# Two attention steps interleaved with projections, and a tail whose weight-gradient sums are turned by DMA

## The chip, the cores and the metric

The kernel runs on one core of one Trainium2 chip, in a single launch. The metric is device time in microseconds: the whole execution, a little longer than the span from the first to the last instruction that the profile draws. Lower is better. Numerals such as L157 are lines of the kernel that was profiled, the one from before the change. Engine names follow the profile: PE is the matrix engine, PEld its weight loads, DVE the vector engine, ACT the scalar engine, POOL and SP the two that issue most of the transfers.

## The reference

Forward and backward pass of window attention over a 256 x 256 image of 384 channels in bfloat16, with windows of 8 x 8 tokens:

```python
qkv = xw @ wqkv                                   # xw: windows of 64 tokens, C = 384
q, k, v = qkv[..., :C], qkv[..., C:2*C], qkv[..., 2*C:]
p = softmax(einsum('bqc,bkc->bqk', q, k) * C ** -0.5, axis=-1)
o = einsum('bqk,bkc->bqc', p, v) @ wo
_, vjp = jax.vjp(forward, x, wqkv, wo)
return out, *vjp(grad_out)                        # out, dx, dwqkv, dwo
```

There are 1024 windows. The outputs are the forward result (out_0), the gradient of x (out_1) and the gradients of the two weight matrices (out_2 and out_3).

## The kernel before, in words

The work is cut into 128 quads. A quad is eight windows in a column, held as four tiles of 128 tokens (two windows each). The weights are first multiplied with each other (A = Wq Wk^T times the scale, B = Wv Wo, and their transposes), so that each token needs four products with 384 x 384 matrices: z from the incoming gradient and BT, y from x and A, u from x and B, v from x and AT.

The main loop runs i from 0 to 128, and each pass is a software pipeline over three quads. In pass i, `step(c, b, a, ahead)` handles c = quad i-1 (its attention), b = quad i (its scores, softmax, u and v) and a = quad i+1 (its z and y). All five engines run in the order in which the program lists their instructions, so the text order of `step` is the order on each engine. It is:

1. `scores(b)`, with the softmax pieces `soft(b, 0..4)` on DVE and ACT between eight `uv` products; ACT copies each u and v out of PSUM (L241).
2. Three z products (`project(a, 0, mo)`, three matmuls of 512 columns each, L157), each copied by ACT into the buffer `yz` (L171); then `soft(b, 5)`.
3. `load(ahead)`: the transfers that fetch a later quad (gradients on POOL's queue, x on SP's).
4. `gather(a, 0)`, a DVE copy of z into `zy` (L179), and three y products, copied by ACT (L173).
5. Up to one row of the weight-gradient sums (`gf_rows`), if a group of three finished quads is waiting in the list `fill`. The list is first filled at the end of pass i = 3.
6. For quads 0 to 3 and the last one, `turn(b)` transposes the probabilities on PE and ACT copies them (L252); for the others DVE does it earlier.
7. `attention(c)`: four tiles (`attend`), one per turn of the generator. A tile is twelve half-size matmuls (L283) into banks called pw, pu, po and pd. One pd product reads `tok`, the z and y of quad c turned to token-major form by a DMA transpose on SP's queue (L183), issued by `to_tokens(sts[i])` at the start of pass i, thus one pass before it is used. Copies out of PSUM: W by DVE on even and ACT on odd tiles in the first passes, U by DVE (L297), o by ACT, d by both (L287); POOL then issues the stores. Once `fill` is in use, sixteen half-size matmuls of weight-gradient sums (`gf_halves`, L338) follow each tile. `gather(a, 1)` comes after the second tile.

PSUM has eight banks, one ring. The next pass's `scores` reads all of `yz`, so PE needs the last y copy of ACT before it can finish the scores.

At SP, every pass issues the DMA transposes dT and xT of quad i+2 (L146), then tok of quad i, then the loads of x.

After the loop, `gf_final` adds the last two quads into the sums `GF_acc` (DVE, L320) and casts them to bfloat16 (`final[0]`, `final[1]`; L349), one row of 128 at a time, a generator that `weight_gradients` draws from. `weight_gradients` then forms the four blocks of the weight gradients from them. Two of the blocks need the sums transposed (`GFT`), which `turn_blocks` does: nine PE transposes (L99) and three copies from PSUM (L91, L93) for each of the two. `product_row` makes one row of a block by three matmuls (L418) and one copy.

Of the kernel before, what the change touches and what calls it, by code (L numbers as in the profile page):

```python
# [11 lines left out]
BF16 = mybir.dt.bfloat16  # L12
F32 = mybir.dt.float32

P = 128
# [8 lines left out]
def kernel(  # L24
# [21 lines left out]
    nc = tc.nc  # L46
    _, H, W, C = x.shape
    CK = C // P
# [5 lines left out]
    grp = ctx.enter_context(tc.tile_pool(name="grp", bufs=2 * GQ + 1))  # L54
# [3 lines left out]
    ring = ctx.enter_context(tc.tile_pool(name="ring", bufs=8, space=bass.MemoryType.PSUM))  # L58
# [13 lines left out]
    def columns(k):  # L72
        return slice(k * C, (k + 1) * C)
# [21 lines left out]
    def turn_blocks(dst, src, first=0, act=True):  # L95
        for k in range(CK):
            pt = ring.tile([P, C], BF16, tag="r", name="pt")
            for m in range(CK):
                nc.tensor.transpose(pt[:, m * P:(m + 1) * P], src[:, m, (first + k) * P:(first + k + 1) * P], ident[:])  # L99
            copy_out(k if act else 0, dst[:, k, :], pt[:])  # L100
# [32 lines left out]
    def load(st):  # L133
        st["xq"] = xq = grp.tile([P, QUAD, C], BF16, tag="xq", name="xq", bufs=2 * GQ + 5)
        st["dq"] = dq = qp.tile([P, QUAD, C], BF16, tag="dq", name="dq", bufs=6)
        for t in range(QUAD):
            nc.gpsimd.dma_start(out=dq[:, t, :], in_=windows(grad_out, st, 2 * t))  # L137
        for t in range(QUAD):
            (nc.gpsimd if st["i"] == AHEAD + 1 else nc.sync).dma_start(out=xq[:, t, :], in_=windows(x, st, 2 * t))
# [21 lines left out]
    def project(st, kind, mo):  # L161
        if kind == 0 and mo == 0:
            st["yz"] = qp.tile([P, CK, QUAD, 4, WT], BF16, tag="yz", name="yz", bufs=1)
        yz = st["yz"]
        wgt, src = ((BT_sb, st["dT"]), (A_sb, st["xT"]))[kind]
        pj = ring.tile([P, QUAD, 2, WT], F32, tag="r")
        for m in range(CK):
            product(pj[:].rearrange("p t w k -> p (t w k)"), wgt[:, m, mo * P:(mo + 1) * P], src[:, :, m, :],
                    m == 0, m == CK - 1)
        if kind == 0:  # L170
            ENG[EV["z"][mo]](out=yz[:, mo, :, 0:4:3, :], in_=pj[:])  # L171
        else:
            ENG[EV["y"][mo]](out=yz[:, mo, :, 1:3, :], in_=pj[:])  # L173
# [24 lines left out]
    def soft(st, step):  # L198
        sd = st["sd"]
        if step == 0:  # L200
            st["mx"] = mx = sm.tile([P, QUAD], F32, tag="mx", name="mx")
            for w, h in ((0, HI), (1, LO)):
                nc.vector.tensor_reduce(out=mx[h, :], in_=sd[h, :, w, :], axis=AX.X, op=ALU.max)
        elif step == 1:
            mx = st["mx"]
            st["sh"] = sh = sm.tile([P, QUAD, WT], F32, tag="sh", name="sh")
            for w, h, o in ((0, HI, LO), (1, LO, HI)):
                nc.vector.tensor_tensor(out=sh[o, :, :], in0=sd[h, :, w, :], in1=over_k(mx[h, :], WT),
                                        op=ALU.subtract)
        elif step == 2:  # L210
            st["ex"] = ex = sm.tile([P, QUAD, WT], F32, tag="ex", name="ex")
            nc.scalar.activation(out=ex[:], in_=st["sh"][:], func=ACT.Exp)
        elif step == 3:
            ex = st["ex"]
            rs = sm.tile([P, QUAD], F32, tag="rs")
            nc.vector.tensor_reduce(out=rs[:], in_=ex[:], axis=AX.X, op=ALU.add)
            ri = sm.tile([P, QUAD], F32, tag="ri")
            nc.vector.reciprocal(out=ri[:], in_=rs[:])
            st["ps"] = ps = qp.tile([P, 2, QUAD, WT], BF16, tag="ps", name="ps")
            st["Pb"], st["dS"] = ps[:, 0, :, :], ps[:, 1, :, :]  # L220
            nc.vector.tensor_tensor(out=st["Pb"], in0=ex[:], in1=over_k(ri[:]), op=ALU.mult)
        elif step == 4:
            st["pr"] = pr = sm.tile([P, QUAD, WT], F32, tag="pr", name="pr")
            for w, h in ((0, LO), (1, HI)):
                nc.vector.tensor_tensor(out=pr[h, :, :], in0=sd[h, :, w, :], in1=st["Pb"][h, :, :], op=ALU.mult)
            st["D"] = D = sm.tile([P, QUAD], F32, tag="D", name="D")
            nc.vector.tensor_reduce(out=D[:], in_=pr[:], axis=AX.X, op=ALU.add)
        else:
            pd = sm.tile([P, QUAD, WT], F32, tag="pd")
            nc.vector.tensor_tensor(out=pd[:], in0=st["Pb"], in1=over_k(st["D"][:]), op=ALU.mult)  # L230
            nc.vector.tensor_tensor(out=st["dS"], in0=st["pr"][:], in1=pd[:], op=ALU.subtract)
# [120 lines left out]
    def attention(st):  # L352
        halves = gf_halves(*fill.pop(0)) if fill else iter(())
        for t in range(QUAD):
            attend(st, t)
            yield
            for k in range(QUAD):
                next(halves, None)

    def step(c, b, a, ahead):  # L360


        def on(st):
            return (lambda f, *r: f(st, *r)) if st is not None else (lambda f, *r: None)
        C_, B, A = on(c), on(b), on(a)
        B(scores)
        B(soft, 0)
        B(uv, 0, 0)
        B(uv, 0, 1)
        B(soft, 1)  # L370
        B(uv, 1, 0)
        B(uv, 1, 1)
        B(soft, 2)
        B(soft, 3)
        B(uv, 2, 0)
        B(uv, 2, 1)
        B(uv, 3, 0)
        B(uv, 3, 1)
        B(soft, 4)
        for mo in range(CK):  # L380
            A(project, 0, mo)
        B(soft, 5)
        if b is not None and not b["on_pe"]:
            turn(b)
        if b is not None and b["i"] == 1:
            turn_blocks(woT_sb, wo_sb, act=False)
        if ahead is not None:
            load(ahead)
        A(gather, 0)
        for mo in range(CK):  # L390
            A(project, 1, mo)
        for rows in range(1 if a is not None else 2):
            if fill:
                gf_rows(*fill.pop(0))
        if b is not None and b["on_pe"]:
            turn(b)
        slots = attention(c) if c is not None else iter(())
        for t in range(QUAD):
            if t == 2:
                A(gather, 1)  # L400
            next(slots, None)
        for rest in slots:
            pass
# [8 lines left out]
    dwo_out = out_3.rearrange("(m p) n -> p m n", p=P)  # L412

    def weight_gradients(group):
        def product_row(k, out, left, right, sc):
            pe = ring.tile([P, C], F32, tag="r", name="pe")
            for m in range(CK):
                nc.tensor.matmul(pe[:], lhsT=left[:, m, k * P:(k + 1) * P], rhs=right[:, m, :],  # L418
                                 start=(m == 0), stop=(m == CK - 1))
            if sc is not None and k % 2:  # L420
                nc.scalar.activation(out=out, in_=pe[:], func=ACT.Copy, scale=sc)
            elif sc is not None:
                nc.vector.tensor_scalar(out=out, in0=pe[:], scalar1=sc, scalar2=None, op0=ALU.mult)
            else:
                copy_out(k, out, pe[:])

        def rows(name):
            return grp.tile([P, CK, C], BF16, tag="xq", name=name, bufs=2 * GQ + 5)

        GFT = [grp.tile([P, CK, C], BF16, tag="Wq", name="GFT") for f in range(2)]  # L430
        for i in range(CK + 1):
            next(group)
        turn_blocks(GFT[0], final[0])
        for i in range(CK - 1):
            next(group)
        for part, left, right in ((0, GFT[0], w_sb[:, :, columns(1)]), (1, final[0], w_sb[:, :, columns(0)])):
            dw = rows("dw")
            for k in range(CK):
                product_row(k, dw[:, k, :], left, right, scale)
            nc.sync.dma_start(out=dw_out[:, :, columns(part)], in_=dw[:])  # L440
        turn_blocks(GFT[1], final[1])
        dwo = rows("dwo")
        for k in range(CK):
            product_row(k, dwo[:, k, :], w_sb[:, :, columns(2)], final[1], None)
        nc.sync.dma_start(out=dwo_out, in_=dwo[:])
        dw = rows("dw")
        for k in range(CK):
            product_row(k, dw[:, k, :], GFT[1], woT_sb, None)
            (nc.sync, nc.scalar)[k % 2].dma_start(out=dw_out[:, k, columns(2)], in_=dw[:, k, :])

    with tc.manual_schedule(engines=MANUAL):
        spare = sm.tile([P, 1], BF16, name="spare", bufs=1)
# [77 lines left out]
```

## Time and profile before

| what | value |
|---|---|
| three timed runs | 1898.62, 1900.75, 1900.82 us (median 1900.75) |
| the profiled execution, its own time | 1902.77 us |
| its span in the profile | 1901.0 us |
| granted PE clock, mean | 0.999 |
| pass i = 2, scores to scores: length, PE busy, ACT busy, DVE busy | 12.73, 11.95, 11.56, 9.85 us |
| pass i = 3: the same | 12.74, 11.95, 11.56, 9.86 us |
| pass i = 4 (the sums now run too): the same | 14.56, 14.56, 11.66, 12.67 us |
| 1887.60 to 1897.30, the products of the tail: length, PE busy, DMA share | 9.70, 9.64 us, 0.19 |

The length of a pass is read in the timeline from the first scores matmul of one pass to the first of the next; the busy times are those of the same stretch. A PE that is busy over a whole stretch leaves no time to be gained from other engines there; where it is less, something makes it wait. The DMA share is the mean busy share of the sixteen transfer engines, with overlapping packets counted twice, so it can pass 1.

### The profile page before, as it was taken

To read this page: it belongs to the slowest core of one execution; us is meant where nothing else is said; L and a number is where in the kernel's file an instruction comes from. 1 tells how busy PE (TensorE), PEld (TensorE's weight loads), DVE (VectorE), ACT (ScalarE), POOL (GpSimd) and SP (SyncE) were. 2 spreads that over 40 slices of the span, in tenths; PEclk is the share of its full clock that TensorE was granted. 3 is DMA by queue.
4 is the path that set the end of the run, shared out by engine and by line. 5 is a ranking of instruction groups with operands and counts; after the bars stand their busy time and mean duration, and the time that the engine had idled before them with its cause. 6 is when DMAs were issued, how large, how long until landed. Compare 5 with 4: busy or idle time off the path is not lost.

```text
span 1901.0 us, 57224 instructions
## 1 busy us (share of the span) xinstructions
PE 1890.5 (99%) x22413; PEld 1128.2 (59%) x22413; DVE 1664.8 (88%) x3606; ACT 1524.7 (80%) x3347; POOL 863.1 (45%) x1576
## 2 busy tenths in 40 slices
PE   9999999999999999999999999999999999999999
PEld 5555565566556655665556655655565566556655
DVE  6888888888888888888888888888888888888887
ACT  7888788878888887888778887888788878888884
POOL 4544454445444444454444444444444445444532
PEclk9999999999999999999999999999999999999999
DMA  9999999999999999999999999999999999999994
GB/s 223 239 219 225 219 217 216 212 224 217 216 221 201 234 216 216 226 216 218 182 231 217 220 220 208 228 209 224 214 216 223 218 207 233 203 230 220 217 185 96
DMA packets 946543, 407.69 MB, mean 214 GB/s; under 512 B 828512, under 2 KB 921696, under 8 KB 946272
## 3 DMA queue, kind: packets, MB, share of 16 engines
q1 hardware_dynamic: 869760, 252.04, 78.4%
q0 software_dynamic: 75264, 151.11, 31.3%
q8 instruction: 175, 2.87, 0.6%
q10 hardware_dynamic: 1248, 0.89, 0.2%
q14 instruction: 96, 0.79, 0.1%
HBM read 101.84 MB, written 101.84 MB: 107 GB/s over the span
## 4 chain that ended last, share of the span: by engine, by line
PE 98%; DMA 1%; DVE 1%; ACT 0%; issue 0%; ACTq 0%; DVEq 0%
PE pj L157 52%; PE pg L157 13%; PE ph L338 13%; PE sd L157 5%; PE pw L283 5%; PE po L283 4%; PE pu L283 4%; DMA tok<-zy 1%; PE pd L283 1%; PE pe L418 0%; DVE Uq L297 0%; PE pc L106 0%; DMA w_sb<-in_wqkv_dram 0%; DVE Wq L294 0%; DVE zy L179 0%; PE pt L99 0%
## 5 line engine op out<-in xcount | busy, mean ns | idle before, releaser
L303 POOL DMA_DIRECT2D out_dram<-o x512 | 273.6, 534 | 918.2 <-ACT o L287 901.9
L294 ACT CAST Wq<-pw 128x384 bf16<-128x384 f32 x506 | 243.4, 481 | 279.5 <-PE pw L283 279.2
L157 PEld LDWEIGHTS <-xT 128*128 128x128 bf16 x3072 | 291.8, 98 | 182.2
L157 PE MATMUL pj<-B_sb,xT 128*128 128x384 bf16 x1536 | 333.4, 326 | 0.0
L157 PE MATMUL pj<-AT_sb,xT 128*128 128x384 bf16 x1536 | 333.3, 326 | 0.0
L137 POOL DMA_DIRECT2D dq<-in_grad_out_dram x508 | 269.1, 542 | 77.7 <-PE pj L157 30.3
L297 DVE CAST Uq<-pu 128x384 bf16<-128x384 f32 x512 | 283.0, 553 | 14.8 <-PE pu L283 2.6
L305 POOL DMA_DIRECT2D out_dram<-d x480 | 278.8, 581 | 15.2 <-ACT uq L241 5.1
L157 PE MATMUL pj<-dT,BT_sb 128*128 128x512 bf16 x1152 | 269.5, 379 | 0.1
L157 PE MATMUL pj<-xT,A_sb 128*128 128x512 bf16 x1152 | 269.5, 379 | 0.0
L283 PE MATMUL pd<-tok,ps 64*64 64x384 bf16 x2048 | 255.1, 327 | 2.3 <-DMA tok<-zy 2.3
L171 ACT CAST yz<-pj 128x512 bf16<-128x512 f32 x384 | 224.3, 585 | 38.4 <-PE pj L157 29.6
L287 ACT CAST o<-po 128x384 bf16<-128x384 f32 x512 | 249.9, 488 | 2.2 <-PE po L283 2.1
L241 ACT CAST vq<-pj 128x384 bf16<-128x384 f32 x512 | 246.6, 482 | 3.6
L241 ACT CAST uq<-pj 128x384 bf16<-128x384 f32 x512 | 243.7, 476 | 3.8 <-PE pj L157 1.9
L173 ACT CAST yz<-pj 128x512 bf16<-128x512 f32 x384 | 224.7, 585 | 24.5 <-PE pj L157 0.6
L258 DVE STREAM_TRANSPOSE PS<-ps 32x256 bf16<-32x256 bf16 x492 | 214.4, 436 | 9.4
L157 PEld LDWEIGHTS <-xq 128*128 128x128 bf16 x1572 | 153.6, 98 | 115.3 <-issue 0.9
L338 PEld LDWEIGHTS <-xq 64*64 64x64 bf16 x6000 | 176.7, 107 | 68.1
L338 PE MATMUL ph<-Wq,xq 64*64 64x384 bf16 x3984 | 204.2, 322 | 0.0
L157 PEld LDWEIGHTS <-A_sb 128*128 128x128 bf16 x1152 | 112.6, 98 | 135.5
L157 PEld LDWEIGHTS <-BT_sb 128*128 128x128 bf16 x1152 | 112.7, 98 | 122.3
(95 smaller groups left out, 3058.2 us busy)
## 6 DMA issues: line engine op xcount, KB each, us to landing
out_dram<-o POOLq DMA_DIRECT2D x512, 96.0 KB, 3.9
xq<-in_x_dram SPq DMA_DIRECT2D x508, 96.0 KB, 4.1
dq<-in_grad_out_dram POOLq DMA_DIRECT2D x508, 96.0 KB, 5.9
out_dram<-d POOLq DMA_DIRECT2D x480, 96.0 KB, 4.3
out_dram<-d POOLq DMA_DIRECT2D x64, 48.0 KB, 4.8
tok<-zy SPq DMA_TRANSPOSE x128, 7.7
xT<-xq SPq DMA_TRANSPOSE x127, 7.5
dT<-dq SPq DMA_TRANSPOSE x126, 7.6
```

What stands on the lines that cost most here:

```text
L137: nc.gpsimd.dma_start(out=dq[:, t, :], in_=windows(grad_out, st, 2 * t))
L157: nc.tensor.matmul(out, lhsT=lhsT, rhs=rhs, start=start, stop=stop)
L171: ENG[EV["z"][mo]](out=yz[:, mo, :, 0:4:3, :], in_=pj[:])
L173: ENG[EV["y"][mo]](out=yz[:, mo, :, 1:3, :], in_=pj[:])
L241: cp(out=dst[:, t, :], in_=pj[:])
L283: nc.tensor.matmul(dst[o, :], lhsT=operand(st, lhs, t, h), rhs=operand(st, rhs, t, h), **flags)
L287: copies[EV[name][i]](out=sb[rows, :], in_=src[rows, :])
L294: copies[EV["W"][t] if st["i"] >= GQ else "DA"[t % 2]](out=st["Wq"][:, t, :], in_=pw[:])
L297: copies[EV["U"][t]](out=st["Uq"][:, t, :], in_=pu[:])
L303: nc.gpsimd.dma_start(out=windows(out_0, st, 2 * t), in_=o)
L305: nc.gpsimd.dma_start(out=windows(out_1, st, 2 * t - 1), in_=d if t else above[:])
L338: nc.tensor.matmul(dst[o, :], lhsT=st["xq"][h, t, ma * P + o.start:ma * P + o.stop], rhs=st["UW"[f] + "q"][h, t, :], start=(i == 0), stop= ...
```

## The change

In passes i = 2 and i = 3 (c is quad 1 or 2) `step` takes a path of its own after `soft(b, 4)`: `load(ahead)` first, then one attention tile of c after each of the three z products and after the first y product; `soft(b, 5)` behind the second z product's tile; `gather(a, 0)` behind the third tile; the other two y products, `turn(b)` and `gather(a, 1)` at the end. Each of the operations that the two passes had is still there, once.

In the tail, each of the two transposed sums is made by one DMA transpose on SP's queue instead of `turn_blocks`. The block that needs no transposed sum is formed first. The last of the twelve rows is formed in two halves of 192 columns, one copied by ACT and the other by DVE, and stored by SP.

```diff
@@ step, after B(soft, 4)
+        if c is not None and c["i"] in (1, 2):
+            load(ahead)
+            slots = attention(c)
+            for mo in range(CK):
+                project(a, 0, mo)
+                next(slots)
+                if mo == 1:
+                    soft(b, 5)
+            gather(a, 0)
+            project(a, 1, 0)
+            next(slots)
+            project(a, 1, 1)
+            project(a, 1, 2)
+            for rest in slots:
+                pass
+            turn(b)
+            gather(a, 1)
+            return
         for mo in range(CK):
             A(project, 0, mo)
@@ weight_gradients
+        def turned(src):
+            dst = grp.tile([P, CK, C], BF16, tag="Wq", name="GFT")
+            nc.sync.dma_start_transpose(out=dst[:].rearrange("p m (k q) -> p (m k) q", q=P),
+                                        in_=src[:].rearrange("p m c -> p (m c)"))
+            return lambda m, k: dst[:, k, m * P:(m + 1) * P]
+
+        def plain(src):
+            return lambda m, k: src[:, m, k * P:(k + 1) * P]
...
-        GFT = [grp.tile([P, CK, C], BF16, tag="Wq", name="GFT") for f in range(2)]
-        for i in range(CK + 1):
+        for i in range(CK):
             next(group)
-        turn_blocks(GFT[0], final[0])
-        for i in range(CK - 1):
+        GFT = [turned(final[0])]
+        for i in range(CK):
             next(group)
-        for part, left, right in ((0, GFT[0], w_sb[:, :, columns(1)]), (1, final[0], w_sb[:, :, columns(0)])):
+        GFT.append(turned(final[1]))
+        for part, left, right in ((1, plain(final[0]), w_sb[:, :, columns(0)]), (0, GFT[0], w_sb[:, :, columns(1)])):
...
-        turn_blocks(GFT[1], final[1])
...
-        for k in range(CK):
+        for k in range(CK - 1):
             product_row(k, dw[:, k, :], GFT[1], woT_sb, None)
             (nc.sync, nc.scalar)[k % 2].dma_start(out=dw_out[:, k, columns(2)], in_=dw[:, k, :])
+        for part, put in ((0, nc.scalar.copy), (1, nc.vector.tensor_copy)):
+            half = slice(part * C // 2, (part + 1) * C // 2)
+            pe = ring.tile([P, C // 2], F32, tag="r", name="pe")
+            for m in range(CK):
+                nc.tensor.matmul(pe[:], lhsT=GFT[1](m, CK - 1), rhs=woT_sb[:, m, half],
+                                 start=(m == 0), stop=(m == CK - 1))
+            put(out=dw[:, CK - 1, half], in_=pe[:])
+        nc.sync.dma_start(out=dw_out[:, CK - 1, columns(2)], in_=dw[:, CK - 1, :])
```

More of the change, by code (lines that the diff above doesn't have):

```diff
@@ L417, in product_row @@
             for m in range(CK):
-                nc.tensor.matmul(pe[:], lhsT=left[:, m, k * P:(k + 1) * P], rhs=right[:, m, :],
+                nc.tensor.matmul(pe[:], lhsT=left(m, k), rhs=right[:, m, :],
                                  start=(m == 0), stop=(m == CK - 1))
@@ L440, in weight_gradients @@
             nc.sync.dma_start(out=dw_out[:, :, columns(part)], in_=dw[:])
-        turn_blocks(GFT[1], final[1])
         dwo = rows("dwo")
         for k in range(CK):
-            product_row(k, dwo[:, k, :], w_sb[:, :, columns(2)], final[1], None)
+            product_row(k, dwo[:, k, :], plain(w_sb[:, :, columns(2)]), final[1], None)
         nc.sync.dma_start(out=dwo_out, in_=dwo[:])
         dw = rows("dw")
-        for k in range(CK):
+        for k in range(CK - 1):
             product_row(k, dw[:, k, :], GFT[1], woT_sb, None)
             (nc.sync, nc.scalar)[k % 2].dma_start(out=dw_out[:, k, columns(2)], in_=dw[:, k, :])
+        for part, put in ((0, nc.scalar.copy), (1, nc.vector.tensor_copy)):
[6 more added lines that the diff above has]
+        nc.sync.dma_start(out=dw_out[:, CK - 1, columns(2)], in_=dw[:, CK - 1, :])
     with tc.manual_schedule(engines=MANUAL):
```

## The prediction, made before the changed kernel ran

> **What bounds the kernel.** I read the chain of waits first: it runs on PE.
>
> ```profile
> PE 98%; DMA 1%; DVE 1%; ACT 0%; issue 0%; ACTq 0%; DVEq 0%
> ```
>
> Then I looked for PE's waits, in the list of PE's waits and the timeline. From pass i = 4 on there is one alone, at 949.8 us, so only passes 1 to 3 and the tail can give anything. Pass i = 2, from scores to scores, reads:
>
> ```profile
> 39.50 0.87 PE L157 MATMUL sd<-xT,yz 128*128 128x64 bf16 x24
> 44.11 2.11 PE L157 MATMUL pj<-dT,BT_sb 128*128 128x512 bf16 x9
> 51.01 0.32 PE L283 MATMUL pw<-dq,ps 64*64 64x384 bf16 x1 [0.23 <-DVE Uq L297]
> 51.95 0.32 PE L283 MATMUL po<-uq,PS 64*64 64x384 bf16 x1 [0.41 <-DVE Wq L294]
> 52.23 0.87 PE L157 MATMUL sd<-xT,yz 128*128 128x64 bf16 x24
> ```
>
> The four tiles run from 48.28 to 52.23, at the speed of the copies; where PE is undisturbed a tile takes 0.49 (pw starts at 76.67, ph behind it at 77.16). Four would take 1.96, so about 2 us are lost here, and as much in pass i = 3. Third, the transfer that feeds those tiles, tok of quad 1, in SP's timeline and in the answer for that transfer (from issue to landing):
>
> ```profile
> 36.75 4.89 SPq L183 DMA_TRANSPOSE tok<-zy  x1
> DMA to landing us min/median/max: 9.7/9.7/9.7
> ```
>
> It lands at 46.45, which is 1.8 before its first use at 48.28. For quad 2 (issued 48.26, 8.8 to landing) it is 57.06 against 61.01. The tail:
>
> ```profile
> 1887.62 0.67 PE L99 MATMUL pt<-ident,GFb 128*128 128x128 bf16 x9
> 1891.52 0.36 DVE L349 CAST GFb<-GF_acc 128x384 bf16<-128x384 f32 x1
> 1893.65 0.67 PE L99 MATMUL pt<-ident,GFb 128*128 128x128 bf16 x9
> 1895.62 1.63 PE L418 MATMUL pe<-woT_sb,GFT 128*128 128x384 bf16 x9
> 1897.28 0.56 DVE L93 CAST dw<-pe 128x384 bf16<-128x384 f32 x1 [0.42 <-PE pe L418]
> ```
>
> PE never stops there: each group of nine transposes costs 0.50 of PE (their start to the next group's).
>
> **Change 1, passes i = 2 and 3.** Nothing is added or removed; PE's sum per pass is scores and u, v 4.61 (39.50 to 44.11), z and y 9 + 9 matmuls at 0.216 = 3.89, the turn 0.31, tiles 1.96: 10.8 against 12.73. At best each pass gains 1.9.
>
> First wait, tok. In pass 2 PE reaches tile 0 after the first z product, 44.11 + 0.65 = 44.76. Everything up to there is as before, on SP too, whose order in these passes isn't changed, so tok lands at 46.45 again: PE waits 1.7 at pd, and behind it stands all of PE, so ACT and DVE run dry as well. In pass 3 tok of quad 2 (57.06) is in time: PE needs it 5.3 after that pass's start, about 58.5.
>
> Second wait, the end of the pass. Today ACT finishes the last o and d under the next pass's scores, which don't need them; now the last y copies come last, and the scores do need them. ACT's spacing when it has a backlog: 0.37 for a 384-column copy (49.16, 49.53, 49.90), 0.48 for one of 512 (the last y copy at 48.20, PS behind it at 48.68). Pass 2 after the wait: PE has tiles 1.96, five products 3.24, turn 0.31 = 5.5, to 52.0. ACT gets its first o at 46.5 + 0.49 + 0.15 = 47.1, and has 4 o, 2 W and 3 d at 0.37 = 3.3 and five z and y at 0.48 = 2.4; with 0.1 for the end of the last and 0.3 to 0.6 where it waits for PE, 53.2 to 53.5. The scores begin in earnest 1.0 to 1.3 later than 52.23; I take 1.2.
>
> That PE stops there is seen at the start of passes 0 and 1, where z and y also come straight before the scores, in the chain:
>
> ```profile
> 25.54 0.59 ACT yz L173
> 26.14 0.05 issue
> 26.18 0.82 PE sd L157 x22
> ```
>
> Pass 3 has no tok wait, but the same end. ACT's z0 copy comes 5.5 after the scores (52.23 to 57.75 today), behind it 6 at 0.48 and 9 at 0.37 = 6.2: 11.8 if it never runs dry, today 12.74. But it does: the second z product ends 0.49 + 0.65 after the first, DVE (four U, two W, two d, `soft(b, 5)`, two gathers: ten at 0.47 and 0.9 = 5.6) holds banks, and each tile's po waits for u's copy. I put 0.5 to 1.3 for it, so -0.4 to +0.4, and take +0.2. What hides today's copies, the next scores and u, v, is gone for y2; DVE's `gather(a, 1)` now follows y2 and holds back the next maximum by 0.5, which PE doesn't wait for (u and v run meanwhile).
>
> POOL issues `dq` before the stores as before; the stores come 2 to 3 earlier, and o has eight buffers. Cost nothing; were a store late by a pass, ACT would wait for it. Passes 4 onward are PE's own, so a shift of the front stays to the end: **+1.4**, between -3.8 (1.9 twice: nothing waits) and +2.5 (all of tok's 1.7 lost, and 0.4 in each pass).
>
> **Change 2, the tail.** Out go 18 PE transposes (2 x 0.50 = -1.0) and six copies, which lay beside PE. In come two DMA transposes of 9 blocks. Nearest row, 12 blocks on a less loaded queue:
>
> ```profile
> 33.35 1.44 SPq L146 DMA_TRANSPOSE dT<-dq  x1
> DMA to landing us min/median/max: 3.8/3.8/3.8
> ```
>
> Bounds: 2.3 (a plain store of the same 288 KB) and 7.6 (the median dT, under load). The tail's DMA share is 0.19, so I go by 3.8 less three blocks; tok's 24 blocks against dT's 12 at their median give only 0.1 for 12, which makes no useful slope, so I take 3.3 to 3.8, 3.5. First transpose: `final[0]` ready 1887.48, lands 1891.0. PE: two sum rows to 1890.39, the plain block 1.46 to 1891.85; hidden, with 0.8 to spare. Second: cast ends 1891.88 - 0.5 = 1891.38, lands 1894.9; PE has block 0 and dwo, 2.92, to 1894.77. Wait 0.1. The last block starts at 1894.9 instead of 1895.62.
>
> The halves: in row 1 ACT copies (0.48), issues a store (0.37 at 1897.30) and only then copies the half row. From the last block's start: row 1 done 0.97 + 0.18, copy 0.49, store issue 0.4, half copy 0.32 (0.48 less 192 columns at 0.84 ns, from 384 and 512 columns' 0.478 and 0.585): 2.4 until SP issues, against 2.25 today. +0.15. Tail: -0.72 + 0.15, **-0.6**, between -0.8 and the third case below.
>
> Sum: +1.4 - 0.6 = **+0.8** on the span of 1901.0, so 1901.8, and 1903.6 for that execution's own 1902.77. Its median companion is 1900.75, 2.0 lower, and the lowest run 1898.62. The reason is in the trace: tok at 936.78 landed 15.27 later, PE stood 2.30, and then a window ran at half clock.
>
> ```profile
> 950.02:953.43 3.41, 1.34 (x31) 0.82 (x32) 1.26 (x3) 0.86 (x2) 0.00 (x0) 1.00 1.06 205
> 953.43:956.85 3.42, 3.42 (x44) 2.24 (x47) 2.13 (x5) 1.82 (x4) 2.48 (x4) 0.50 1.18 260
> ```
>
> (Columns: length, busy of PE, PEld, DVE, ACT, POOL, granted clock, DMA share, GB/s.) 2.3 + 1.7 = 4.0, about 1902.77 - 1898.62: a late transfer that not every run has. The forecast is the median plus 0.8: **1901.5**.
>
> **Rivals.**
> A. *The copies do hide* (faster). Both passes reach PE's sum: -3.8, tail -0.6: 1896.4. For it: with a backlog ACT needs 17 copies at 0.37, 7 at 0.48 and 0.3 for the exponential, 10.0, and DVE is busy 9.85; both are under 10.8. Against: tok's landing, and y2 last.
> B. *Half of that*: pass 2 loses its 1.2, pass 3 gains 1.9: -1.3, 1899.4. For it: in pass 3 only the order of the copies stands in the way.
> C. *The turned sums are late* (slower). One mechanism: the transposes take the loaded 7.6. The first lands 1895.1, PE waits 3.2 and ends dwo at 1898.0; the second lands 1899.0, the last block starts 3.4 later than today; tail +3.5, total 1905.7. It decides from about 4.0 for the second transpose, where the tail stops gaining. Against: the idle queue. The Trainium skill (VectorE: DVE Perf Modes, The three transpose paths) prefers TensorE where PSUM will do, 390 ns a block, and puts the DMA path at 1309 ns; nine in a row would be an estimate of 11.8, both behind each other on one queue, the last block 15.5 late, 1918. The row of 12 blocks in 3.8 speaks against blocks in a row.
> D. *The new wait halves the clock*. 1.7 of standing in pass 2 is followed by a 3.4 window at 0.50, as above: +1.7, 1903.2. Against: the window before that one had PE busy 1.34 of 3.41; 1.7 of waiting leaves half or more. The Trainium skill (TensorE: Matmul & The Clock Gate, Part 1: The HAM clock gate) asks for an idle window of about 3.4 us, free-running; by that no gate closes here, though at 949.8 a 2.3 wait was enough.
>
> **How the numbers follow.** Forecast 0.58, A 0.10, B 0.12, C 0.10, D 0.10. The forecast's own range is 1900.5 to 1902.2 (pass 2 +1.0 to +1.3, pass 3 -0.4 to +0.4, tail -0.8 to -0.3); runs with and without the late transfer differ by 2.2, so 1898.3 to 1904.4 holds it with B and D, and leaves out A and C. What a measurement can tell from no change is about 0.2%, 3.8 us: beyond it lie on the fast side A (0.10), on the slow side C and D with a late transfer on top (0.13); the rest, 0.77, is no change.
>
> **What would show it.** Right: a PE wait at pd for tok of 1.5 to 1.9 near 44.8 to 46.5; scores of pass 4 starting 1.0 to 2.0 later than 64.97, waiting for ACT yz; passes after that at 14.57; the transposes of GFb landing in 3 to 4; the last block's first matmul 5.4 to 5.7 before the end (today 5.4). Wrong: no wait for tok, passes under 12, or a wait over 1 at GFT.

## The result, and the profile after

The changed kernel's median is 1901.49 us (22 runs, 1899.08 to 1905.87). The kernel before, run beside it on the same chip, has 1898.68 (22 runs, 1898.11 to 1901.54). The ratio is 1.0016, with a 95% interval of 1.0009 to 1.0022: some 3.0 us slower (1.7 to 4.2), which is within what was called no change, but on its slow side and clear of zero. The forecast of 1901.5 agrees with the time only because two errors cancel. It stood on a median of three runs, 1900.75, two of which were untypical (18 of the 22 runs of the kernel before lie between 1898.1 and 1899.3), and it added 0.8 where 2.8 was right. That the two errors met is luck.

The profiled execution has a span of 1901.0 us, just as the one before. But that of before had lost time to a late transfer at 949.8. The pass that holds it goes from one of these scores to the other:

```profile
938.90 0.87 PE L157 MATMUL sd<-xT,yz 128*128 128x64 bf16 x24
958.00 0.87 PE L157 MATMUL sd<-xT,yz 128*128 128x64 bf16 x24
```

It takes 19.10, where the passes around it take 14.57, thus 4.5 more (the prediction had reckoned 4.0). Without it, 1896.5 is what the new span should be held against. The chain of waits gives the same picture as before:

```profile
PE 98%; DMA 1%; DVE 0%; ACT 0%; issue 0%; ACTq 0%
```

So PE's waits are next. These are two lines of the list of what PE waited for: total us, times, longest.

```profile
PE pd L283 <- DMA tok<-zy: 3.2, 1, 3.2
PE sd L157 <- ACT yz L173: 0.6, 2, 0.3
```

The first is a transfer, the second the y copy at the end of the two changed passes. The timeline of PE says where they lie (start, duration, what ran; in brackets the idle time before it and its cause):

```profile
40.14 0.87 PE L157 MATMUL sd<-xT,yz 128*128 128x64 bf16 x24
...
45.51 0.35 PE L283 MATMUL pd<-tok,ps 64*64 64x384 bf16 x2
...
52.33 0.38 PE L157 MATMUL sd<-xT,yz 128*128 128x64 bf16 x2
52.99 0.82 PE L157 MATMUL sd<-xT,yz 128*128 128x64 bf16 x22 [0.28 <-ACT yz L173]
...
61.81 0.53 PE L283 MATMUL pd<-tok,ps 64*64 64x384 bf16 x2 [3.18 <-DMA tok<-zy]
...
69.75 0.55 PE L157 MATMUL sd<-xT,yz 128*128 128x64 bf16 x2
70.58 0.81 PE L157 MATMUL sd<-xT,yz 128*128 128x64 bf16 x22 [0.28 <-ACT yz L173]
...
85.08 0.87 PE L157 MATMUL sd<-xT,yz 128*128 128x64 bf16 x24
```

A pass is the distance from one start of the scores (`sd`) to the next. Pass 2 takes 52.33 - 40.14 = 12.19, pass 3 takes 17.42, pass 4 takes 15.33; before, they were 12.73, 12.74 and 14.56. Pass 3 holds a wait of 3.18 at pd, and no wait stands in pass 2, where the prediction had put one. (The 0.6 is 0.28 in front of the 22 late scores of pass 3 and 0.28 in front of those of pass 4. What follows the scores, the first u product, starts 0.71 after their start in pass 2, 1.31 in pass 3 and 1.48 in pass 4.) SP's timeline and the answer for the transfer that PE waited for, tok of quad 2:

```profile
36.52 4.20 SPq L183 DMA_TRANSPOSE tok<-zy  x1
47.74 7.01 SPq L183 DMA_TRANSPOSE tok<-zy  x1
```

```profile
DMA to landing us min/median/max: 14.0/14.0/14.0
```

It was issued at 47.74, half a us earlier than before, and took 14.0 where it had taken 8.8. What moved most in its time are the stores. The first of pass 2, in POOL's timeline, starts 6.89 after that pass's first scores (first line); before, it was 10.45 after (second line, from the profile before):

```profile
47.03 0.55 POOL L303 DMA_DIRECT2D out_dram<-o  x1 [0.44 <-ACT o L287]
49.95 0.54 POOL L303 DMA_DIRECT2D out_dram<-o  x1 [2.92 <-ACT o L287]
```

The last part of pass 3 is the clock. These are two windows in a row; the columns are length, busy time of PE, PEld, DVE, ACT and POOL, granted clock, DMA share, GB/s:

```profile
58.19:61.61 3.42, 0.44 (x2) 0.10 (x1) 0.83 (x2) 0.62 (x2) 0.52 (x1) 1.00 1.05 185
61.61:65.02 3.41, 3.21 (x26) 1.02 (x26) 1.58 (x3) 1.09 (x3) 1.08 (x2) 0.50 1.21 248
```

PE was busy for 0.44 of the first, and in the second it got half the clock. Pass 3 is 5.23 longer than pass 2, and the timeline splits this in three. The scores are 0.60 late. From their late end to the first pd it takes 3.51 more (the 3.18 of the list counts only from the end of the product before). From pd to the end of the pass it takes 69.75 - 61.81 = 7.94, where pass 2 takes 52.33 - 45.51 = 6.82; these 1.12 hold the window at half clock, which thus cost less than the 1.7 that half of a whole window would be.

The tail, in the timeline:

```profile
1888.55 5.18 SPq L435 DMA_TRANSPOSE GFT<-GFb  x2
...
1892.70 1.63 PE L445 MATMUL pe<-w_sb,GFT 128*128 128x384 bf16 x9
...
1894.16 1.62 PE L445 MATMUL pe<-GFb,w_sb 128*128 128x384 bf16 x9
...
1895.72 1.15 PE L445 MATMUL pe<-woT_sb,GFT 128*128 128x384 bf16 x6
...
1896.70 0.66 PE L480 MATMUL pe<-woT_sb,GFT 128*128 128x192 bf16 x6
...
1897.41 0.36 ACTq L475 DMA_DIRECT2D out_dram<-dw  x1
...
1897.82 0.32 ACT L482 CAST dw<-pe 128x192 bf16<-128x192 f32 x1 [0.44 <-ACT dw L91]
1898.16 0.34 SPq L483 DMA_DIRECT2D out_dram<-dw  x1
```

The two transposes were issued 3.90 apart and each landed after 3.2, at 1891.8 and 1895.7. PE came to the first sum at 1892.70, after it had landed, and to the second at 1895.72. That is 1.56 after the block before it, where the blocks ahead are 1.46 apart, so PE lost 0.10. From the last pass's scores to the end it is 38.93, against 39.93 before.

The clock column of the single runs says how often the windows at half clock come. One such window in a span of 1900 takes the mean clock to 0.999. Of the 22 runs of the changed kernel 11 have 0.999 or less, with a median of 1902.82; the other 11 have 1.000 and 1901.05, still 2.4 above the kernel before, so the clock is the smaller part of the loss. Of 111 runs of the kernel before, made beside the experiments, 8 have 0.999 or less.

### The profile page after: what moved, and what is told of

It is laid out like the page before. It is cut to its first block, busy times and chain, and to the rows that moved or that the text cites. A ratio compares the mean times of both kernels' runs of the same rounds, so it can differ in the third digit from the quotient of the medians.

```text
span 1901.0 us, 57195 instructions
## 1 busy us (share of the span) xinstructions
PE 1891.0 (99%) x22398; PEld 1125.1 (59%) x22398; DVE 1662.6 (87%) x3602; ACT 1523.0 (80%) x3346; POOL 861.8 (45%) x1576
## 4 chain that ended last, share of the span: by engine, by line
PE 98%; DMA 1%; DVE 0%; ACT 0%; issue 0%; ACTq 0%
PE pj L157 52%; PE pg L157 13%; PE ph L338 13%; PE sd L157 5%; PE pw L283 5%; PE po L283 4%; PE pu L283 4%; DMA tok<-zy 1%; PE pd L283 1%; PE pe L445 0%; PE pc L106 0%; PE warm L87 0%; PE pt L99 0%; ACT yz L173 0%; DVE Uq L297 0%; PE pt L153 0%
```

## The experiments

They run from the two halves of the change to the transfers. The time beside each is the median; "before" is the kernel before on the same chip.

**The tail alone (e1), and the passes alone (e2).** First the new tail without the path in `step`, then that path with the old tail:

```diff
-        if c is not None and c["i"] in (1, 2):
+        if c is not None and c["i"] in ():
```

> The tail of the change alone; passes i = 2 and 3 as before. Late-tok theory (the loss is PE waiting at pd for the transfer tok in passes 2 and 3, and the half clock that can follow): about 0.7 us faster than before, no PE wait at pd in passes 2 and 3, runs as close together as those of before. Rival 'the turned sums are late': slower than before by up to 3 us, PE waiting at a product that reads GFT. Rival 'last y copy': as the first.

> The interleaved passes alone; tail as before. Late-tok theory: 3 to 4 us slower than before in the median, runs spread over some 6 us, and in the profile the time of passes 2 and 3 beyond before's 25.5 equals PE's wait at pd for tok plus about 1.7 for each window at half clock. Rival 'last y copy': slower by a fixed 1 to 2 us, with PE waiting for ACT yz at the two scores, whatever tok does.

The tail alone gives 1897.46 against 1898.75 before, 0.9995 (0.9987 to 1.0004); 10 of 11 runs lie between 1896.9 and 1898.1, and its tail measures 38.94, 1.0 shorter. The interval doesn't show the gain, but the same 38.93 to 38.97 stands in the profile of each of the twelve kernels with the new tail, and 39.93 and 39.94 in the two with the old. The passes alone give 1901.82, 1.0013 (1.0004 to 1.0022): they carry the whole loss. In their profile PE waits 1.78 for tok of quad 2, which took 12.6, and these are the window that holds that wait and the one behind it:

```profile
57.05:60.47 3.42, 1.64 (x16) 0.57 (x15) 1.62 (x4) 1.06 (x3) 0.34 (x1) 1.00 1.37 251
60.47:63.88 3.41, 3.41 (x18) 0.80 (x16) 2.53 (x6) 2.29 (x5) 1.37 (x3) 0.50 0.97 213
```

**tok issued first (e3, e4).** In passes 1 and 2, SP issues tok of quad i, which the next pass reads, ahead of dT and xT of quad i+2; once in the changed kernel, once with the old order of `step` (both with the new tail).

```diff
+            if i in (1, 2):
+                to_tokens(sts[i])
             load_turn(...)
-            if 0 <= i < n:
+            if 0 <= i < n and i not in (1, 2):
                 to_tokens(sts[i])
```

> The changed kernel, with tok issued ahead of the transposes dT and xT in passes 1 and 2, so that it goes out some 3 to 5 us earlier on SP's queue. Late-tok theory: no wait at pd in passes 2 and 3, no half clock, 2.5 to 4 us faster than the changed kernel, 0 to 1 us faster than before; spread of runs as before's. Rival 'last y copy': only the tok part goes, still 1 us or more slower than before. A new wait could come at the z products of passes 2 and 3, which read dT.

> As the run before this one (tok first, new tail), but with passes 2 and 3 in the order of before. Tells what the interleaving is worth when tok is not late. Late-tok theory with the copies as the bound: the same time as with the interleaving within 1 us, about 0.7 us faster than before, passes 2 and 3 at 12.7 each. If interleaving hides the copies: 2 to 4 us slower than the interleaved one.

The changed kernel comes to 1901.66, 1.0016 (1.0007 to 1.0024), the plain one to 1898.96, 1.0000 (0.9991 to 1.0009), 1.5 more than the tail alone. Nothing was won. PE's waits in the changed kernel with tok first:

```profile
PE pd L283 <- DMA tok<-zy: 2.4, 2, 2.2
PE pj L157 <- DMA dT<-dq: 2.4, 2, 2.0
PE pj L157 <- DMA xT<-xq: 0.8, 1, 0.8
```

The longest ones came later in the queue: 2.0 for dT of quad 4, which now stood behind tok of quad 2, and 2.2 for tok of quad 3. (The 0.8 for xT and the other 0.4 for dT lie in passes 0 and 1, ahead of the edit.) In the plain one tok of quad 2 took 13.4, without early stores, while dT and xT moved beside it. This speaks for a shortage in the whole stream of these passes, and not in one place of the queue. The two long waits left the clock alone: the windows around them have PE busy 1.96 and more.

```profile
56.77:60.19 3.42, 1.96 (x13) 0.98 (x10) 2.29 (x6) 2.46 (x7) 2.33 (x5) 1.00 1.28 175
60.19:63.60 3.41, 2.90 (x31) 1.06 (x32) 1.68 (x4) 1.74 (x4) 0.55 (x1) 1.00 1.15 248
77.25:80.66 3.41, 2.34 (x14) 1.13 (x12) 1.04 (x3) 0.68 (x2) 0.00 (x0) 1.00 1.19 124
80.66:84.08 3.42, 2.14 (x47) 1.32 (x51) 2.14 (x4) 1.34 (x3) 0.55 (x1) 1.00 1.22 242
```

**The stores held (e5), and the last tile behind y (e8).** POOL collects the stores of quads 1 and 2 and issues them at the end of the pass's text, behind a small POOL copy that reads the first y copy. The second version also moves the fourth tile behind the last y product, so that the y copies no longer come last.

```diff
+    def store(st, out, in_):
+        if st["i"] in (1, 2):
+            late.append((out, in_))
+        else:
+            nc.gpsimd.dma_start(out=out, in_=in_)
...
-        nc.gpsimd.dma_start(out=windows(out_0, st, 2 * t), in_=o)
+        store(st, windows(out_0, st, 2 * t), o)
...
             project(a, 1, 0)
-            next(slots)                 # second version alone
...
             gather(a, 1)
+            nc.gpsimd.tensor_copy(out=spare[:], in_=a["yz"][:, 0, 0, 1, 0:1])
+            for out, in_ in late:
+                nc.gpsimd.dma_start(out=out, in_=in_)
+            late.clear()
             return
```

> The changed kernel, with POOL's stores of passes 2 and 3 held back until the first y copy of the pass, some 10 us after its scores, where they stood before the change; everything else as changed. 'Early stores' theory (the stores of o and d, now 3 us earlier, share the transfer engines with tok of quad 2 and make it take 13 to 14 us instead of 9): tok of quad 2 takes 8 to 10 again, no or under 1 us of PE wait at pd in pass 3, no half clock, 2.5 to 4 us faster than the changed kernel, 0.5 to 1 faster than before. Rival 'tok is just needed too early': tok of quad 2 still 12 or more, PE waits 1 us or more in pass 3, still 2 us slower than before. In both PE waits some 0.4 for ACT yz at each of the two following scores.

> As the first of these four (stores held), and the fourth tile goes behind the third y product instead of the first, so that ACT copies y2 before that tile's o and d. If the last y copy holds the scores, PE's waits for ACT yz go, passes 2 and 3 take 11.3 to 12.0 each, and the kernel is 2 to 3 us faster than before. If the two passes are bound by their copies alone, 12.2 to 12.7 each and no gain over the first of the four.

With the stores held, tok of quad 2 lands in 6.3 instead of 14.0:

```profile
DMA to landing us min/median/max: 6.3/6.3/6.3
```

This execution flatters it, for in it PE had stood in pass 2 (below), which may have left the transfers more time. The second version had no such wait: there the first store of pass 2 starts 10.63 after the scores, close to the 10.45 of before, and tok of quad 2 takes 8.3, close to the 8.8 of before. So in this order it is the early stores that lengthen it, as far as one execution each can show. The time is still 1901.48, 1.0007 (0.9996 to 1.0018), in two groups: 4 runs at 1898.0 to 1898.8 and 8 at 1901.05 and above. The profile is one of the upper group, and there it is tok of quad 1, which PE meets in pass 2, that comes late; PE's waits and the window:

```profile
PE pd L291 <- DMA tok<-zy: 2.5, 1, 2.5
```

```profile
47.68:51.09 3.41, 1.39 (x18) 0.50 (x19) 0.99 (x2) 0.48 (x1) 1.03 (x2) 1.00 1.18 201
```

That is the wait that the prediction had in pass 2, and the half-clock window of its rival D behind it. It was there in this execution and not in that of the changed kernel, although the program ahead of it is the same: it is a matter of the single run.

The second version has the lowest ratio of the study, 0.9988 (0.9978 to 0.9998). Its median is 1897.9 against 1898.78: 0.9 less, where the tail alone has 1.3 less, so the medians show no gain from the passes. PE in its profile:

```profile
39.67 0.87 PE L157 MATMUL sd<-xT,yz 128*128 128x64 bf16 x24
...
51.48 0.87 PE L157 MATMUL sd<-xT,yz 128*128 128x64 bf16 x24
...
63.28 0.87 PE L157 MATMUL sd<-xT,yz 128*128 128x64 bf16 x24
...
77.84 0.87 PE L157 MATMUL sd<-xT,yz 128*128 128x64 bf16 x24
...
92.41 0.87 PE L157 MATMUL sd<-xT,yz 128*128 128x64 bf16 x24
...
104.75 0.35 PE L291 MATMUL pd<-tok,ps 64*64 64x384 bf16 x2 [1.46 <-DMA tok<-zy]
...
109.23 0.87 PE L157 MATMUL sd<-xT,yz 128*128 128x64 bf16 x24
```

The 24 scores run in one piece, no y copy is waited for, and passes 2 to 4 take 11.81, 11.80 and 14.56, in sum 38.17 where the kernel before has 40.03: 1.9 gained, half of the 3.8 that PE's sum allowed. The last three lines show where it went: in pass 6 PE waits 1.46 for tok of quad 5, which took 13.0, and the pass takes 16.82, 2.3 more than its neighbours. In this execution the front's gain was lost again, and more.

**One pass alone (e6, e7).** The condition becomes `c["i"] == 2` (pass 3 alone) and `c["i"] == 1` (pass 2 alone).

> The changed kernel with pass 2 in the order of before; pass 3 interleaved; new tail. 'Early stores': pass 2's stores are where they were, so tok of quad 2 takes 8 to 10 and PE waits under 0.5 in pass 3; 0.5 to 1 faster than before. 'Needed too early': PE waits 1 us or more at pd in pass 3 and the time is 1 us or more over that of the tail alone.

> The changed kernel with pass 3 in the order of before; pass 2 interleaved; new tail. 'Early stores': tok of quad 2 takes 12 to 14, but is needed 3.4 later, so a wait at pd in pass 3 of 0 to 1; about the time of the tail alone, up to 1 over it. 'Needed too early': no wait at all, tok at 8 to 10.

Medians 1898.38, 0.9994 (0.9984 to 1.0004), and 1899.16, 0.9998 (0.9987 to 1.0008). With the new tail worth -1.0 in both, either pass alone costs nothing to 1.4. It doesn't settle which of the two carries the loss. The profiles do say how the stores bear on tok of quad 2: 14.2 where pass 2 stores early, 11.3 where it stores as before. With pass 3 alone, PE waits 1.9 for it, and the window behind this one has half the clock:

```profile
57.75:61.16 3.41, 1.51 (x16) 0.57 (x15) 1.50 (x4) 0.93 (x3) 1.84 (x4) 1.00 1.16 251
```

**Without reading tok (e9).** In quads 1 and 2 the product that reads `tok` reads the tiles dq and xq instead, which are there long before; that part of out_1 is another value then.

```diff
     def operand(st, n, t, h):
...
+        if n in ("z", "y") and st["i"] in (1, 2):
+            return st[{"z": "dq", "y": "xq"}[n]][h, t, :]
```

> The changed kernel, in which the attention of quads 1 and 2 takes the two tok operands from the tiles of the gradient and of x that the same attention tile reads anyway, so it waits for no turned z and y (those two quads' part of out_1 is not the reference's). Same matmuls, same copies; tok is still moved. Late-tok theory: no wait at pd in passes 2 and 3, passes 12.2, 12.2 and 15.3, no half clock, 3 to 4 us faster than the changed kernel, about 1.3 faster than before, runs as close together as before's. Rival 'the copies and the last y are the loss': still 1 us or more slower than before.

Its profiled execution has no wait for a transfer at all, and a span of 1895.4 (1897.15 in time, the fastest of its runs). Its passes 2 to 4 take 12.19, 12.79 and 15.16, in sum 40.14, as long as before's 40.03: with nothing late, this order of tiles gains nothing, since each pass ends in the wait for y. But the median of the 12 runs is 1900.35, 1.0010 (0.9997 to 1.0022), up to 1912.01. So the theory that the reading of tok in passes 2 and 3 is the whole loss falls. The clock column agrees: the run of 1912.01 has 0.997 and that of 1903.6 has 0.999, so PE stood somewhere in them too.

**Other orders (e10, e11).** One puts all three z products first and a tile behind each y product; the other puts z and the first y product first.

```diff
             for mo in range(CK):
                 project(a, 0, mo)
-                next(slots)
-                if mo == 1:
-                    soft(b, 5)
+            soft(b, 5)
+            next(slots)                 # second version: behind project(a, 1, 0)
             gather(a, 0)
-            project(a, 1, 0)
-            next(slots)
-            project(a, 1, 1)
-            project(a, 1, 2)
+            for mo in range(CK):        # second version: a tile behind the middle one alone
+                project(a, 1, mo)
+                next(slots, None)
```

> Computes all. In passes 2 and 3 the three z products come first, then the tiles, each behind which one y product: tile 0 needs tok 1.3 us later than in the changed kernel, and y2 stands ahead of the fourth tile. Late-tok theory: waits at pd rarer and smaller than in the changed kernel but not gone, passes 11.5 to 12.0 without a wait; median 1 to 2 us faster than before, with some runs 3 slower. If the loss had been in the copies alone: every run 2 faster than before.

> Computes all. As the one above, but a y product more ahead of tile 0, which needs tok 1.9 us later than in the changed kernel and 1.6 earlier than before; stores come 1.6 earlier than before. Late-tok theory: hardly a wait, passes 11.6 to 12.0, 2 to 3 us faster than before in the median and the least spread of all interleaved kernels.

They come to 1899.97, 1.0002 (0.9993 to 1.0010), with waits of 0.4, 1.3 and 0.6 at pd, and 1900.21, 1.0009 (0.9999 to 1.0019), whose profiled execution, at 1896.7 the second fastest, lists no wait of PE for a transfer and has passes 2 to 4 of 38.57 in sum, 1.6 less than e9's, but whose runs go from 1896.23 to 1907.22. In an execution where nothing is late, a tile behind the last y product is thus worth what the wait for y had cost; over all runs the gain is not there.

**Without reading tok, quads 1 to 9 (e12).** The same edit as above, for nine quads.

> As the kernel that read no tok for quads 1 and 2, but for quads 1 to 9 (those quads' part of out_1 is not the reference's). The time of that one stayed spread from 1897 to 1912 although passes 2 and 3 could not wait for tok. 'The wait moves to a later tok' (PE, being earlier, uses up what the transfers had to spare, and stands at tok in passes 4 to 10 instead): now nearly all runs within 1 us of 1897.3, 1.3 to 1.5 faster than before. Rival 'it moves to another transfer' (dT or xT in front of the projections): the runs stay spread over 5 us or more, the median 1 us or more above before, and a slow execution's profile has PE waiting for dT or xT.

The median is 1901.77, 1.0006 (0.9997 to 1.0016). No product of these quads reads tok any more, and still PE stands. DVE's timeline in pass 4, and PE's:

```profile
79.40 0.56 DVE L179 COPY zy<-yz 128x1536 bf16<-128x1536 bf16 x1 [3.38 <-DMA tok<-zy]
80.00 0.56 DVE L322 TENSOR_TENSOR GF_acc<-pg,GF_acc 128x384 f32<-128x384 f32 x1
```

```profile
80.61 0.32 PE L285 MATMUL pw<-dq,ps 64*64 64x384 bf16 x1 [2.31 <-DVE GF_acc L322]
```

The transfer tok of quad 3 was still made, took 13.8, and still read the buffer `zy`. DVE's gather of the next z had to wait 3.38 for that buffer, the sum `GF_acc` stood behind it on DVE and held a bank, and PE waited 2.31 for the bank. PE's list of waits names DVE there, but the cause is the transfer. So neither expectation holds as it was put: the time doesn't fall to 1897.3, and PE waits for neither dT nor xT. The clock followed:

```profile
77.90:81.31 3.41, 0.99 (x24) 0.45 (x20) 1.84 (x4) 0.63 (x2) 0.55 (x1) 1.00 1.19 232
81.31:84.72 3.41, 3.41 (x49) 2.62 (x45) 2.34 (x5) 2.00 (x5) 1.92 (x3) 0.50 1.18 176
```

**What the runs say together.** The stream of transfers in the first passes has little to spare. Before the change, tok of quads 1 to 4 landed 1.8, 4.0, 6.1 and 7.9 before its first use; in the changed kernel's profile it is 0.0, none (3.18 late), 7.2 and 12.0, the last two only because PE had stood. The interleaving takes from this twice: PE needs tok some 3.4 earlier in the pass (8.78 after its start before, 5.37 in pass 2 now), and the stores, which come 3.5 earlier too, lengthen it from about 9 to between 11 and 15. The profiles show executions that lose nothing, a wait, or a wait and a halved window; which of these a given run meets seems to be decided by small differences between runs. The middle twelve of the 22 runs of the changed kernel cover 1.85 us, those of the kernel before 0.65. (The extremes tell less: among the runs of the kernel before that stand beside the experiments, single ones reach 1906.39.)

Left open: only one run of each kernel was profiled, so where the late ones of e9, e10 and e11 stood is not shown. The profiles show where the single executions lost their time; that late transfers make up the whole 3 us of the medians is argued from them. Holding the stores alone left the median at 1901.48, and reading no tok left it at 1900.35 and 1901.77. The one version that brought it back, to 1897.9, holds the stores and moves the fourth tile as well; between it and the held stores alone lies only that tile's place, worth 3.6 in the medians, of which the wait for y explains 2.0 (passes 2 to 4 of 40.14 in e9 against 38.17). Nor was it tried whether lighter traffic in the first passes makes the 1895 to 1896 of the best single runs the rule.

## Why the prediction was right and wrong

**Bound, right for this kernel.** PE sets the time, and in the changed kernel's profile every pass from 5 on takes the 14.57 of before. That a gain of the front stays to the end did not hold everywhere: pass 6 takes 16.82 in the profile of the held stores with the last tile behind y, 16.02 with z first and 15.56 with tok first.

**Tail, right in mechanism, too small.** -0.6 was forecast, -1.0 measured. The transposes landed in 3.2, not 3.5, the first was hidden and the second cost 0.10, as said. The mis-sized term is PE's own time: the two sum rows were put to end at 1890.39, but they take 2.60 (1888.13 to 1890.73 before), which from 1887.62 gives 1890.22. So the last block came 0.91 earlier and not 0.72. The halves do delay the last issue (2.44 after the last block's start, against 2.25: the +0.15), but the end came 5.28 after that start instead of 5.38, since the last transfer landed in 1.64 and not 1.80, and what follows its landing took 1.20 and not 1.33. Rival C is out: the loaded 7.6 didn't occur on that idle queue. The Trainium skill (VectorE: DVE Perf Modes, The three transpose paths) gives 1309 ns a block, from which 11.8 for nine would be an estimate. The trace has nine blocks in 3.2, and the measurement decides.

**Pass 2, wrong in the profiled run.** "PE waits 1.7 at pd" rested on SP being as before, so that tok lands at 46.45 again. It landed at 45.46, just as PE came, and there was no wait. Single executions differ by more than the reserve: from that pass's start tok took 6.99 before, 5.33 after, 8.11 with the stores held, where the wait was there with 2.45.

**The y copies, right in kind, too large.** The scores do wait for ACT's last y. Forecast +1.2 in pass 2 against today's end; measured, from the first u product of pass 2 to that of pass 3, 12.79 against 12.74, thus next to nothing. The estimate had put ACT's copies behind a PE that had waited 1.7: its first o at 47.1, 7.6 after the scores. Without that wait it came after 6.1, which probably is the difference.

**Pass 3, the step that failed.** "tok of quad 2 (57.06) is in time" took the transfer's time from a trace in which the stores came later, and "the stores come 2 to 3 earlier ... Cost nothing" looked only at who issues them and how many buffers there are. I didn't ask what they share the transfer engines with. The runs show 14.0 instead of 8.8, a PE wait of 3.18 that puts pd 3.51 late, and 1.1 more behind it, with the halved clock: passes 2 to 4 are 4.9 longer, where the front was put at +1.4, +0.2 of it for pass 3. The spans agree: 1896.5, 0.6 because pass 2 started later in this execution (40.14 against 39.50, with the same program ahead of it), 4.9 and -1.0 make the measured 1901.0. In the medians the front costs 3.1 (the passes alone against before), since not each run waits as long.

**Rivals.** A stood on the copies and B on the same gain in pass 3; e9 shows that with y last the front gains nothing even with no late transfer, and the version with the last tile behind y shows that half of it is there, 1.9 in passes 2 to 4, although its pass 6 lost it again. D named the right mechanism, a wait that halves the clock, in the wrong pass; it deserved more than 0.10, as half of the runs have a mean clock that fits it.

## What to carry to other kernels

Moving work forward moves its transfers and its needs forward too: before an edit, list for each transfer how long before its first use it lands, and take off what the consumer gains and what earlier stores on other queues add. Here a median of three runs lay 2 us from that of twenty-two, more than an edit of this size is worth. And where PE waits for another engine, ask what that engine had waited for: a late transfer can come in by a buffer that it still reads.

## What was unexpected of the hardware

The clock halves after far less than an idle window. In windows of 3.41 us inside the main loop, PE busy 0.44, 0.99, 1.34, 1.39, 1.51 or 1.64 was followed by one at 0.50, and 1.96, 2.14 or 2.34 was not, though waits of 1.97 and 2.23 lay in or across those. A wait of 2.23 that straddles two windows was free of it where one of 1.78 inside a window was not. Busy time alone doesn't draw the line, though: at the end of the launch, where PE stops for good, windows with 1.58 (pass 3 alone), 1.62 (z first) and 1.73 (before) were followed by full clock. What sets these apart from the 1.64 is not shown. These are the first of the three and the window behind it:

```profile
1894.12:1897.53 3.41, 1.58 (x13) 0.96 (x12) 1.47 (x3) 0.84 (x3) 0.00 (x0) 1.00 0.80 262
1897.53:1899.37 1.84, 0.00 (x0) 0.00 (x0) 0.00 (x0) 0.00 (x0) 0.00 (x0) 1.00 0.08 28
```

The Trainium skill (TensorE: Matmul & The Clock Gate, Part 1: The HAM clock gate) asks for at least one idle window of about 3.4; the waits here were 1.78 to 3.18, so the measurement goes against it on that point.

One and the same DMA transpose of 24 blocks, tok of quad 2, took 6.3 and 8.3 with the stores held back, 8.8 to 11.3 with the stores at their old place and 11.3 to 14.6 with them early. The ranges meet, and with tok first it took 13.4 beside dT and xT without early stores, so plain stores on another queue are one cause of its length, and not the only one.
